# Two equal stationary pieces of 64 columns for the state update and the logits of a scan with two mixtures of experts

## The chip, the cores and the metric

The kernel runs on one core of one Trainium2 chip, in one launch. The metric is the device time of the whole program in microseconds (us), and the median of several runs is quoted. The core's engines are TensorE (PE, with its weight loads shown apart as PEld), VectorE (DVE), ScalarE (ACT), GpSimd (POOL) and SyncE (SP, which issues the transfers here).

## The reference

Three stages follow each other: a linear recurrence with a complex gate (`attn`), a dense two-layer map with a piecewise quadratic function (`moe`), and eight experts with weights from a balanced softmax (`moe2`).

```python
# attn: B, H, S, D = 4, 8, 768, 48; a is scaled so that |a| <= 0.999
for t in range(S):
    new_re = ar * S_re - ai * S_im
    new_im = ar * S_im + ai * S_re
    kv = np.einsum('bhd,bhe->bhde', k[:, :, t], v[:, :, t])
    S_re, S_im = (new_re + kv, new_im)
    y[:, :, t] = np.einsum('bhd,bhde->bhe', q[:, :, t], S_re)
# moe: 3072 tokens, d_model 384, d_ff 2048
h = x @ w_in
g = np.where(h >= 1, h, np.where(h <= -1, 0.0, (h + 1) ** 2 / 4))
x = g @ w_out
# moe2: 8 experts, d_ff 1024
P = np.exp(x @ w_gate - max)      # then 8 rounds of row and column scaling
out = sum over e of P[:, e:e + 1] * (np.maximum(x @ w1[e], 0) @ w2[e])
```

## The kernel before

The 768 steps are cut into six chunks of 128, and the four batches into two pairs; a chunk of one pair is a unit `u`, so there are twelve. A unit has 16 heads (8 for each batch of the pair).

For a unit the front part (`attn_norm`, `attn_front`) scales the gates and forms their running products along time: it turns them with transposes (`tA`), runs a scan of complex products on VectorE (`Pk`, `M`), turns them back (`tP`) and makes scaled queries `qh` and keys `kh` (96 values a head: 48 real, 48 imaginary). The back part (`attn_back`) then works like chunked linear attention:

- `turn(g)` transposes four heads of `kh` and `qh` (`kTps`, `qTps`), and ScalarE copies them out;
- `score(g)` makes the 128x128 scores of four heads (`sc`), and VectorE masks them into `at`;
- `value(g)` makes the output `y` of four heads, from the carried state `Tst` (line 385, not in the first chunk) and from `at` and the values `v` (line 389). Its 128 rows of output are made as two pieces of 64 (`halves`);
- `state(b)` (lines 393 to 402) makes what the chunk adds to the state, `z`, for the 8 heads of one batch: the head's 96 columns of `kh` are the stationary operand, as a piece of 64 and one of 32, and the head's 48 values `v` move. `z` is then added to `Tst`, by ScalarE's copy in the first chunk and by VectorE after that. The last chunk has no state update, which leaves ten units with two blocks each.

At the end of a unit `y` is transposed (`x0ps`) and split into a high and a low part, `x0h` and `x0l`. `moe1(u)` takes them through the first mixture: layer 1 into `h` (line 123), the quadratic on ScalarE and VectorE (`t`, then `gh` and `gl`), layer 2 into `x2pa` and `x2pb` (line 513). Then, for each of three chunks `m` of the model dimension, ScalarE copies 128x256 results out (`x2b`), a transfer stores them, and two matmuls (one for each batch) add to the logits `lg` (line 526), with 128 columns of `x2b` as the stationary and 8 of `w_gate` moving. VectorE copies `lg` to `P`.

`weave` draws pieces of the attention of later units between the matmuls of `moe1(u)`, and a scheduler that sees priorities sets the final order on each engine at build time. Float32 weights of the first mixture arrive as raw words in three staging buffers (`stg`); VectorE repacks them (`st_m`), and a pair of matmuls (`lo`) helps split them. After the twelve units the eight experts run on TensorE (`eh` at line 123, `o` at line 657) to the end. PSUM tiles of the attention and of `lg` share the pool `psp` with three buffers.

Of the kernel before, what the change touches and what calls it, by code (L numbers as in the profile page):

```python
# [9 lines left out]
F32 = mybir.dt.float32  # L10
# [10 lines left out]
def scan_moe_moe(  # L21
# [14 lines left out]
    nc = tc.nc  # L36
    B, H, S, D = q.shape
# [3 lines left out]
    T = 128  # L41
    NCH = S // T
    KC = DM // 128
    NF1 = F1 // 128
    NF2 = F2 // 128
    BH = 2
    NU = NCH * (B // BH)
    HU = BH * H
    CU = BH * DM
    G = CU // 128  # L50
    D2 = 2 * D
# [38 lines left out]
    wg = const.tile([128, KC, NE], F32, name="wg")  # L90
# [7 lines left out]
    def f32(ap):  # L98
        return ap.bitcast(F32)
# [54 lines left out]
            )  # L154
            yield

    # ------------------------------------------------------------------
    # phase 1 pools
    # ------------------------------------------------------------------
    ph1 = ctx.enter_context(ExitStack())  # L160
    wpb = ph1.enter_context(tc.tile_pool(name="wpb", bufs=NF1 - 12))
    x0p = ph1.enter_context(tc.tile_pool(name="x0p", bufs=3))
# [1 line left out]
    ap1 = attn.enter_context(tc.tile_pool(name="ap1", bufs=1, side="right"))  # L164
# [70 lines left out]
    def parts(u):  # L235
        return [(b, 1) for b in range(BH)] if u < NSPLIT else [(0, BH)]

    front = {}

    def attn_front(u):  # L240
        c, bp = divmod(u, B // BH)
        A, qn, kn, vn = (loaded.pop((u, nm)) for nm in "aqkv")
        PN = ap1.tile([128, 2, CU], F32, name=f"PN{u}", tag="PN")
        Pk = ap1.tile([128, 2, G, T], F32, name=f"Pk{u}", tag="Pk")
        M = ap1.tile([128, 2, 2, G, T // 2], F32, name=f"M{u}", tag="s12")
        n12 = ap1.tile([128, 2, CU], F32, name=f"n12_{u}", tag="s12")
        qh = ap1.tile([128, HU, 2, D], F32, name=f"qh{u}", tag="qh")
        kh = ap1.tile([128, HU, 2, D], F32, name=f"kh{u}", tag="kh")
        front[u] = (qh, kh, vn)
        tiles = (A, qn, kn, Pk, M, PN, n12, qh, kh)  # L250
        yield from both(*[front_part(u, c, bp, b0, nb, *tiles) for b0, nb in parts(u)])

# [90 lines left out]

    def attn_back(u):
        c, bp = divmod(u, B // BH)
        qh, kh, vn = front.pop(u)
        qf = qh.rearrange("p h i d -> p h (i d)")
        kf = kh.rearrange("p h i d -> p h (i d)")
        alt = ps_a if u == 0 else psp
        ys = [ap1.tile([128, DM], F32, name=f"ysb{u}_{b}", tag="ysb", bufs=2) for b in range(BH)]  # L350
        NG = HU // 4
        halves = (slice(0, 64), slice(64, 128))
        kqT, ats = {}, {}

        def turn(g):
            tt = []
            for nm, src in (("kT", kf), ("qT", qf)):
                ps = alt.tile([128, 4, 128], F32, name=f"{nm}ps{u}_{g}", tag="m")
                for i in range(4):
                    nc.tensor.transpose(ps[:D2, i, :], src[:, 4 * g + i, :], ident)  # L360
                t = ap1.tile([128, 4, 128], F32, name=f"{nm}{u}_{g}", tag=nm, bufs=2)
                nc.scalar.activation(t[:D2], ps[:D2], AF.Copy)
                tt.append(t)
            kqT[g] = tt

        def score(g):
            kT, qT = kqT[g]
            ps = psp.tile([128, 4, 128], F32, name=f"sc{u}_{g}", tag="m")
            for i in range(4):
                nc.tensor.matmul(ps[:, i, :], kT[:D2, i, :], qT[:D2, i, :], start=True, stop=True)  # L370
            at = ap1.tile([128, 4, 128], F32, name=f"at{u}_{g}", tag="at", bufs=2)
            nc.vector.tensor_tensor(
                out=at, in0=ps, in1=mask.unsqueeze(1).to_broadcast([128, 4, 128]), op=ALU.mult
            )
            ats[g] = at

        def value(g):
            at = ats.pop(g)
            qT = kqT.pop(g)[1]
            yps = psp.tile([128, 4, D], F32, name=f"y{u}_{g}", tag="m")  # L380
            for i in range(4):
                h = 4 * g + i
                if c:
                    for o in halves:
                        nc.tensor.matmul(  # L385
                            yps[o, i, :], qT[:D2, i, o], Tst[:D2, bp * HU + h, :], start=True, stop=False
                        )
                for o in halves:
                    nc.tensor.matmul(yps[o, i, :], at[:, i, o], vn[:, h, :], start=(c == 0), stop=True)  # L389
            o = g % 2 * 4 * D  # L390
            nc.scalar.activation(ys[g // 2][:, o:o + 4 * D], yps.rearrange("p h d -> p (h d)"), AF.Copy)

        def state(b):
            zps = psp.tile([128, H, D], F32, name=f"z{u}_{b}", tag="m")
            for h in range(b * H, (b + 1) * H):
                for o in (slice(0, 64), slice(64, D2)):
                    nc.tensor.matmul(zps[o, h - b * H, :], kf[:, h, o], vn[:, h, :], start=True, stop=True)  # L397
            tv = Tst[:D2, bp * HU + b * H:bp * HU + (b + 1) * H, :]
            if c == 0:
                nc.scalar.activation(tv, zps[:D2], AF.Copy)  # L400
            else:
                nc.vector.tensor_tensor(out=tv, in0=zps[:D2], in1=tv, op=ALU.add)

        turn(0)
        yield 1
        for g in range(NG + 1):
            if g + 1 < NG:
                turn(g + 1)
                yield 1
            if g < NG:  # L410
                score(g)
                yield 1
            if g:
                value(g - 1)
                yield 1
                if g % 2 == 0 and c < NCH - 1:
                    state(g // 2 - 1)
                    yield 1
        xh = x0p.tile([128, KC, UT], F32R, name=f"x0h{u}", tag="x0h")
        xl = x0p.tile([128, KC, UT], F32R, name=f"x0l{u}", tag="x0l")  # L420
        for kcs in ((0, 1), (2,)):
            ps = psp.tile([128, 2, UT], F32, name=f"x0ps{u}_{kcs[0]}", tag="m")
            for kc in kcs:
                for b in range(BH):
                    nc.tensor.transpose(
                        ps[:, kc - kcs[0], b * T:(b + 1) * T], ys[b][:, kc * 128:(kc + 1) * 128], ident
                    )
            n = len(kcs)
            oh = xh[:, kcs[0]:kcs[0] + n, :]
            ol = xl[:, kcs[0]:kcs[0] + n, :]  # L430
            nc.scalar.activation(oh, ps[:, :n], AF.Copy)  # L431
            nc.vector.tensor_tensor(out=ol, in0=ps[:, :n], in1=f32(oh), op=ALU.subtract)  # L432
        x0[u] = (xh, xl)
        yield 1
# [42 lines left out]
    def moe1(u):  # L477
# [4 lines left out]
        for p in range(NP + LAG1):  # L482
# [19 lines left out]
            if p >= LAG1:  # L502
                gh, gl = hh.pop(p - LAG1)
                for i in range(2):
                    j = 2 * (p - LAG1) + i
                    w = wm[j]
                    for m in range(KC):
# [4 lines left out]
                        for n, (s, g) in enumerate(((0, gh), (0, gl), (1, gh))):  # L512
                            nc.tensor.matmul(  # L513
                                acc[m], w2p(w, s, m * 128, 128), g[:, i, :],
                                start=(j == 0 and n == 0 and m != 1), stop=(j == NF1 - 1 and n == 2 and m != 0),
                                skip_group_check=(m < 2),
                            )
                    yield 1
        lg = psp.tile([128, BH, NE], F32, name=f"lg{u}", tag="m")
        for m in range(KC):  # L520
            with tc.high_priority(60):
                xb = x0p.tile([128, UT], F32, name=f"x2b{u}_{m}", tag="x2b", bufs=2)
                nc.scalar.activation(xb, acc[m], AF.Copy, scale=0.25)
                nc.sync.dma_start(x2s[c][:, m, bp * UT:(bp + 1) * UT], xb)
            for b in range(BH):
                nc.tensor.matmul(  # L526
                    lg[:, b, :], xb[:, b * T:(b + 1) * T], wg[:, m, :],
                    start=(m == 0 and b == 0), stop=(m == KC - 1 and b == BH - 1), skip_group_check=True,
                )
        j = c * B + bp * BH  # L530
        nc.vector.tensor_copy(P[:, j:j + BH, :], lg)
        yield 1
# [20 lines left out]
    def both(*gs):  # L553
        gs = list(gs)
        while gs:
            for g in list(gs):
                try:
                    yield next(g)
                except StopIteration:
                    gs.remove(g)  # L560
# [41 lines left out]
    load_qkv(0)  # L602
    drain(attn_norm(0))
    drain(attn_front(0))
    side = chain(*[step(u) for u in range(NU)])
    for u in range(NU):
# [7 lines left out]
        weave(moe1(u), side, RATIO)  # L614
    ph1.close()

    # ------------------------------------------------------------------
    # phase 2
    # ------------------------------------------------------------------
    xrp2 = main.enter_context(tc.tile_pool(name="xrp2", bufs=1, side="right", reuse_waits="tile"))  # L620
    accp = main.enter_context(tc.tile_pool(name="accp", bufs=1, reuse_waits="tile"))
    acc = accp.tile([128, NTT, DM], F32, name="acc")
# [73 lines left out]
    for n in range(len(steps) + LAG):  # L696
        if n < len(steps):
            i, f = steps[n]
# [8 lines left out]
        if n >= LAG:  # L707
            i, f = steps[n - LAG]
# [8 lines left out]
                            j = units[r][1] * B + b  # L717
                            nc.vector.tensor_scalar_mul(acc[:, j, :], acc[:, j, :], P[:, j, 0:1])

    # ------------------------------------------------------------------  # L720
    # inputs outside the ranges that the path above covers
    # ------------------------------------------------------------------
    st = const.tile([128, 4], F32, name="st")
    nc.vector.tensor_reduce(out=st[:, 0:1], in_=mins, axis=AX.X, op=ALU.min)
    nc.vector.reduce_max(out=st[:, 1:2], in_=wst[:, 0], axis=AX.XY)
# [235 lines left out]
```

## Time and profile before

| | us |
|---|---|
| median of 3 runs | 2410.22 |
| lowest, highest | 2409.65, 2413.41 |
| span of the profiled execution | 2408.3 |
| PE busy | 2344.7 |
| DVE busy | 1075.6 |
| ACT busy | 806.6 |
| POOL busy | 1.4 |

The results name no other time for the profiled execution than its span, from the first to the last instruction. A busy time is the union of the records of an engine; PE records overlap, since matmuls are pipelined, so the pace of a row of matmuls is read from the start of one to the start of the next and not from their durations. Each float32 matmul of the program leaves two records. A row of the timeline merges neighbours of one kind: its start, its length, the engine, the line, the tile, the shape of the array used (rows*columns of the stationary), the operand, and the number of records.

### The profile page before, as it was taken

The numbers are of one execution on the slowest core, as the hardware profiler recorded it, in microseconds if no ns is written. First come the engines' busy times: TensorE is split into PE (matmuls) and PEld (weight loads), VectorE is DVE, ScalarE is ACT, GpSimd is POOL, SyncE is SP. The second block draws the span as 40 slices with busy tenths as digits, with TensorE's granted clock in tenths as the row PEclk, the third lists the DMA queues.
The fourth block names the chain that finished last, engine by engine and source line by source line (L and its number), as shares of the span: only waits on it lengthen the run. The fifth ranks groups of instructions, "written<-read, shape, count | busy, mean of one in ns | idle before, by whom it ended". The sixth has DMA issues, their size and how long they took to land.

```text
span 2408.3 us, 34837 instructions
## 1 busy us (share of the span) xinstructions
PE 2344.7 (97%) x14957; PEld 2133.0 (89%) x14957; DVE 1075.6 (45%) x2060; ACT 806.6 (33%) x1405; POOL 1.4 (0%) x14
## 2 busy tenths in 40 slices
PE   4899999999999999999999999999999999999998
PEld 3679999999999898999999999999999999999997
DVE  7788877776665783322322232232232223222222
ACT  5677776665567211211211121121121112111111
POOL 0000000000000000000000000000000000000000
PEclk8999999999999999999999999999999999999999
DMA  6442222221103330100100010010010001000000
GB/s 131 138 93 47 40 41 40 42 45 35 34 15 125 112 133 13 53 1 1 46 7 1 14 40 1 1 53 1 1 47 7 1 16 38 1 1 7 27 27 28
DMA packets 186163, 90.42 MB, mean 38 GB/s; under 512 B 128400, under 2 KB 181136, under 8 KB 186000
## 3 DMA queue, kind: packets, MB, share of 16 engines
q1 hardware_dynamic: 186000, 88.11, 13.9%
q8 instruction: 119, 1.95, 0.3%
q14 instruction: 44, 0.36, 0.1%
HBM read 78.66 MB, written 9.44 MB: 37 GB/s over the span
## 4 chain that ended last, share of the span: by engine, by line
PE 90%; DVE 4%; DMA 3%; ACT 2%; issue 1%; SPq 0%; DVEq 0%; ACTq 0%
PE eh L123 32%; PE o L657 31%; PE h L123 8%; PE x2pa L513 5%; PE z L397 3%; PE x2pb L513 2%; PE sc L370 2%; DMA raw<-in_moe_w_in_dram 2%; PE y L385 1%; PE y L389 1%; PE lo L472 1%; PE qTps L360 1%; PE kTps L360 1%; DVE M L282 1%; PE lg L526 1%
## 5 line engine op out<-in xcount | busy, mean ns | idle before, releaser
L123 PE MATMUL eh<-x2h,w_e 128*128 128x512 f32 x2304 | 783.3, 394 | 0.0
L657 PE MATMUL o<-w_e,eg 128*128 128x384 f32 x3072 | 780.5, 334 | 0.7 <-DVE acc L667 0.7
L643 DVE SCALAR_TENSOR_TENSOR el<-eh,eg 128x512 fp32r<-128x512 f32 x384 | 264.9, 690 | 895.9 <-ACT eg L642 895.9
L642 ACT ACTIVATE eg<-eh 128x512 fp32r<-128x512 f32 x384 | 229.6, 598 | 1248.1 <-PE eh L123 1229.2
L657 PEld LDWEIGHTS o<-w_e,eg 128*128 128x128 f32 x3072 | 560.7, 188 | 35.9 <-issue 0.9
L657 PE MATMUL o<-w_e,el 128*128 128x384 f32 x1536 | 513.8, 335 | 0.0
L123 PEld LDWEIGHTS eh<-x2h,w_e 128*128 128x128 f32 x2304 | 432.9, 188 | 83.8
L123 PE MATMUL eh<-x2l,w_e 128*128 128x512 f32 x1152 | 456.9, 397 | 0.0
L657 PEld LDWEIGHTS o<-w_e,el 128*128 128x128 f32 x1536 | 288.4, 188 | 0.0
L123 PEld LDWEIGHTS eh<-x2l,w_e 128*128 128x128 f32 x1152 | 216.2, 188 | 34.7
L123 PE MATMUL h<-x0h,w_m 128*128 128x256 f32 x1152 | 233.1, 290 | 1.0 <-ACT x0h L431 0.5
L123 PEld LDWEIGHTS h<-x0h,w_m 128*128 128x128 f32 x1152 | 186.9, 192 | 3.7 <-issue 1.1
L513 PE MATMUL x2pa<-gh,w_m 128*128 128x256 f32 x768 | 179.7, 295 | 9.3 <-ACT gh L498 9.3
L123 PE MATMUL h<-x0l,w_m 128*128 128x256 f32 x576 | 163.7, 284 | 0.1
L671 DVE SCALAR_TENSOR_TENSOR acc<-o,P,acc 128x384 f32<-128x384 f32 x168 | 95.5, 611 | 128.7 <-PE o L657 128.7
L513 PEld LDWEIGHTS x2pa<-gh,w_m 128*128 128x128 f32 x768 | 134.6, 193 | 13.1 <-ACT gh L498 11.0
L123 PEld LDWEIGHTS h<-x0l,w_m 128*128 128x128 f32 x576 | 110.8, 192 | 0.5 <-DVE x0l L432 0.3
L513 PE MATMUL x2pa<-gl,w_m 128*128 128x256 f32 x384 | 111.2, 289 | 0.1
L513 PE MATMUL x2pb<-gh,w_m 128*128 128x256 f32 x384 | 101.5, 284 | 0.0
L110 DVE TENSOR_TENSOR w_e<-st_e,w_e 128x768 fp32r<-128x768 f32 x64 | 61.1, 957 | 79.9 <-ACT w_e L109 79.9
L492 ACT ACTIVATE t<-h,c_one 128x512 f32<-128x512 f32 x96 | 65.8, 685 | 56.8 <-PE h L123 49.0
L109 ACT ACTIVATE w_e<-st_e 128x768 fp32r<-128x768 f32 x64 | 53.9, 844 | 79.1 <-PE o L657 75.6
(135 smaller groups left out, 2184.2 us busy)
## 6 DMA issues: line engine op xcount, KB each, us to landing
st_e<-in_moe_w_dram SPq DMA_DIRECT2D x128, 192.0 KB, 2.6
st_m<-in_moe_w_in_dram SPq DMA_DIRECT2D x16, 384.0 KB, 3.6
st_m<-in_moe_w_out_dram SPq DMA_DIRECT2D x16, 384.0 KB, 4.2
raw<-in_moe_w_in_dram SPq DMA_DIRECT2D x16, 384.0 KB, 3.5
raw<-in_moe_w_out_dram SPq DMA_DIRECT2D x16, 384.0 KB, 4.0
q<-in_q_dram SPq DMA_DIRECT2D x12, 384.0 KB, 4.0
k<-in_k_dram SPq DMA_DIRECT2D x12, 384.0 KB, 3.7
v<-in_v_dram SPq DMA_DIRECT2D x12, 384.0 KB, 3.7
```

Source lines behind the costliest of these rows:

```text
L109: nc.scalar.activation(w[:, 0, :], st, AF.Copy)
L110: nc.vector.tensor_tensor(out=w[:, 1, :], in0=st, in1=f32(w[:, 0, :]), op=ALU.subtract)
L123: nc.tensor.matmul(ps, w1p(w, s, kc), x[:, kc, :], start=(n == 0), stop=(n == 3 * KC - 1))
L360: nc.tensor.transpose(ps[:D2, i, :], src[:, 4 * g + i, :], ident)
L370: nc.tensor.matmul(ps[:, i, :], kT[:D2, i, :], qT[:D2, i, :], start=True, stop=True)
L397: nc.tensor.matmul(zps[o, h - b * H, :], kf[:, h, o], vn[:, h, :], start=True, stop=True)
L492: nc.scalar.activation(t, ps, AF.Relu, bias=c_one, scale=-0.25)
L513: nc.tensor.matmul(acc[m], w2p(w, s, m * 128, 128), g[:, i, :], start=(j == 0 and n == 0 and m != 1), stop=(j == NF1 - 1 and n == 2 and m ...
L642: nc.scalar.activation(xh, ps, AF.Relu)
L643: nc.vector.scalar_tensor_tensor(out=xl, in0=ps, scalar=0.0, in1=f32(xh), op0=ALU.max, op1=ALU.subtract)
L657: nc.tensor.matmul(po[i, b], g[:, b * T:(b + 1) * T], w2p(w, s, 0, DM), start=(f == 0 and n == 0), stop=(f == NF2 - 1 and n == 2),)
L671: nc.vector.scalar_tensor_tensor(out=a, in0=ps, scalar=P[:, j, e:e + 1], in1=a, op0=ALU.mult, op1=ALU.add)
```

## The change

The stationary operand of the state update becomes two pieces of 64 columns a head. The second piece begins at the head's column 64 and goes 32 columns past its end, into the next head's columns; the results of those 32 columns land in partitions 96 to 127 of `z`, which nothing reads. For the last head the tile of `kh` is 32 columns longer, and GpSimd clears these with a memset for each unit. The logits' matmuls are cut in two along the tokens, 64 columns of `x2b` each. The rest of the diff replaces comments by blank lines.

```diff
         qh = ap1.tile([128, HU, 2, D], F32, name=f"qh{u}", tag="qh")
-        kh = ap1.tile([128, HU, 2, D], F32, name=f"kh{u}", tag="kh")
-        front[u] = (qh, kh, vn)
+        khx = ap1.tile([128, HU * D2 + 32], F32, name=f"kh{u}", tag="kh")
+        nc.gpsimd.memset(khx[:, HU * D2:], 0.0)
+        kh = khx[:, :HU * D2].rearrange("p (h i d) -> p h i d", h=HU, i=2)
+        front[u] = (qh, khx, vn)
...
-        qh, kh, vn = front.pop(u)
+        qh, khx, vn = front.pop(u)
         qf = qh.rearrange("p h i d -> p h (i d)")
-        kf = kh.rearrange("p h i d -> p h (i d)")
+        kf = khx[:, :HU * D2].rearrange("p (h m) -> p h m", h=HU)
...
             for h in range(b * H, (b + 1) * H):
-                for o in (slice(0, 64), slice(64, D2)):
-                    nc.tensor.matmul(zps[o, h - b * H, :], kf[:, h, o], vn[:, h, :], start=True, stop=True)
+                for o in halves:
+                    ko = khx[:, h * D2 + o.start:h * D2 + o.stop]
+                    nc.tensor.matmul(zps[o, h - b * H, :], ko, vn[:, h, :], start=True, stop=True)
...
             for b in range(BH):
-                nc.tensor.matmul(
-                    lg[:, b, :], xb[:, b * T:(b + 1) * T], wg[:, m, :],
-                    start=(m == 0 and b == 0), stop=(m == KC - 1 and b == BH - 1), skip_group_check=True,
-                )
+                for o in (0, 64):
+                    nc.tensor.matmul(
+                        lg[o:o + 64, b, :], xb[:, b * T + o:b * T + o + 64], wg[:, m, :],
+                        start=(m == 0 and b == 0), stop=(m == KC - 1 and b == BH - 1), skip_group_check=True,
+                    )
```

TensorE at the first state update of unit 7, between two layer-2 pieces of unit 6, before the change (a row gives the line, the tile written, the operands and the shape of the output; a number behind a name is the unit, the last one a buffer):

```order
L513 MATMUL x2pb6_5474<-gl6_3_5546,w_m6_707 128x256
L513 MATMUL x2pb6_5474<-gh6_3_5545,w_m6_707 128x256
L397 MATMUL z7_0_5737<-v7_4574,kh7_4607 64x48
L397 MATMUL z7_0_5737<-v7_4574,kh7_4607 32x48
...
L513 MATMUL x2pa6_5473<-gh6_3_5545,w_m7_733 128x256
L513 MATMUL x2pa6_5473<-gl6_3_5546,w_m7_733 128x256
```

The same place after the change:

```order
L516 MATMUL x2pb6_5519<-gl6_3_5591,w_m6_708 128x256
L516 MATMUL x2pb6_5519<-gh6_3_5590,w_m6_708 128x256
L400 MATMUL z7_0_5782<-v7_4611,kh7_4644 64x48 x16
L516 MATMUL x2pa6_5518<-gh6_3_5590,w_m7_734 128x256
L516 MATMUL x2pa6_5518<-gl6_3_5591,w_m7_734 128x256
```

The block stands where it stood, with 16 matmuls as before; the eight of 32 columns have become eight of 64.

TensorE at the logits of unit 6, which stand among the first layer-1 matmuls of unit 7, before:

```order
L123 MATMUL h7_0_6042<-x0h7_5946,w_m0_531 128x256
L526 MATMUL lg6_6012<-wg_96,x2b6_0_6013 128x8 x2
L123 MATMUL h7_0_6042<-x0h7_5946,w_m0_531 128x256
L123 MATMUL h7_0_6042<-x0l7_5947,w_m0_531 128x256
L526 MATMUL lg6_6012<-wg_96,x2b6_1_6018 128x8 x2
L123 MATMUL h7_0_6042<-x0h7_5946,w_m0_531 128x256 x2
```

and after:

```order
L123 MATMUL h7_0_6093<-x0h7_5991,w_m0_532 128x256
L530 MATMUL lg6_6057<-wg_96,x2b6_0_6058 64x8 x4
L123 MATMUL h7_0_6093<-x0h7_5991,w_m0_532 128x256
L530 MATMUL lg6_6057<-wg_96,x2b6_1_6065 64x8 x4
L123 MATMUL h7_0_6093<-x0l7_5992,w_m0_532 128x256
```

Two matmuls of 128 columns have become four of 64, and the second group stands one layer-1 matmul earlier. Elsewhere on TensorE and VectorE some neighbours change places by one or a few instructions. GpSimd has twelve memsets more, each waiting for TensorE's last use of the unit before; VectorE's write of `kh` waits for GpSimd besides, and so does the last matmul of a unit's second state block.

## Rows read from the trace of the kernel before

**Rows 1.** Page: busy time of engines, and the chain by engine and line

```profile
PE 2344.7 (97%) x14957; PEld 2133.0 (89%) x14957; DVE 1075.6 (45%) x2060; ACT 806.6 (33%) x1405; POOL 1.4 (0%) x14
...
PE 90%; DVE 4%; DMA 3%; ACT 2%; issue 1%; SPq 0%; DVEq 0%; ACTq 0%
PE eh L123 32%; PE o L657 31%; PE h L123 8%; PE x2pa L513 5%; PE z L397 3%; PE x2pb L513 2%; PE sc L370 2%; DMA raw<-in_moe_w_in_dram 2%; PE y L385 1%; PE y L389 1%; PE lo L472 1%; PE qTps L360 1%; PE kTps L360 1%; DVE M L282 1%; PE lg L526
```

**Rows 2.** Waits of PE, 200 to 700 us: total, times, longest

```profile
PE h L123 <- DVE t L495: 0.2, 1, 0.2
```

**Rows 3.** Timeline of PE, first state block of unit 7: start, length

```profile
505.67 3.65 PE L397 MATMUL z<-v,kh 128*64 128x48 f32 x32
509.25 0.39 PE L513 MATMUL x2pa<-gh,w_m 128*128 128x256 f32 x1
```

**Rows 4.** Windows around the twenty z blocks, z alone: first window and sum

```profile
57.90:62.00 4.10, 3.62 (x32) 2.63 (x32) 0.00 (x0) 0.15 (x1) 1.00 0.00 0
...
sum 79.70, PE 73.06 PEld 52.66 DVE 1.56 ACT 0.50; mean PE 3.65 PEld 2.63 DVE 0.08 ACT 0.02
```

**Rows 5.** Timeline of PE, a y block of unit 7 with its neighbours

```profile
493.64 0.28 PE L513 MATMUL x2pb<-gh,w_m 128*128 128x256 f32 x1
493.85 0.32 PE L385 MATMUL y<-Tst,qT 96*64 96x48 f32 x4
...
494.70 0.29 PE L389 MATMUL y<-v,at 128*64 128x48 f32 x4
494.92 0.39 PE L123 MATMUL h<-x0h,w_m 128*128 128x256 f32 x1
495.14 0.28 PE L123 MATMUL h<-x0l,w_m 128*128 128x256 f32 x1
```

**Rows 6.** Windows after three z blocks; the granted clock follows POOL's entry

```profile
224.70:227.80 3.10, 3.10 (x17) 3.06 (x16) 2.95 (x5) 0.05 (x1) 0.00 (x0) 0.53 0.64 126
285.50:289.00 3.50, 3.50 (x18) 3.44 (x18) 2.50 (x5) 1.34 (x3) 0.00 (x0) 0.52 0.57 112
509.20:512.70 3.50, 3.50 (x31) 3.45 (x30) 3.34 (x8) 1.59 (x3) 0.00 (x0) 1.00 0.02 5
```

**Rows 7.** Timeline of PE, a logits group among layer-1 matmuls

```profile
474.57 0.28 PE L123 MATMUL h<-x0l,w_m 128*128 128x256 f32 x1
474.69 0.51 PE L526 MATMUL lg<-wg,x2b 128*128 128x8 f32 x4
475.05 0.48 PE L123 MATMUL h<-x0h,w_m 128*128 128x256 f32 x2
475.37 0.28 PE L123 MATMUL h<-x0l,w_m 128*128 128x256 f32 x1
```

**Rows 8.** Chain in unit 0; timeline of DVE and PE in unit 1

```profile
58.37 3.44 PE z L397 x32
...
64.45 3.42 PE z L397 x32
...
69.53 0.68 PE lo L472 x2
...
166.34 0.69 DVE L372 TENSOR_TENSOR at<-sc,mask 128x512 f32<-128x512 f32 x1 [1.98 <-PE sc L370]
...
172.52 0.69 DVE L432 TENSOR_TENSOR x0l<-x0ps,x0h 128x512 fp32r<-128x512 f32 x1 [1.32 <-ACT x0h L431]
...
179.93 1.50 PE L263 MATMUL tP<-ident,Pk 128*128 128x128 f32 x12 [0.41 <-DVE Pk L291]
```

**Rows 9.** Timeline of DVE and PE around the two z blocks of unit 7

```profile
509.36 0.55 DVE L402 TENSOR_TENSOR Tst<-z,Tst 96x384 f32<-96x384 f32 x1 [0.40 <-PE z L397]
...
513.05 0.69 DVE L372 TENSOR_TENSOR at<-sc,mask 128x512 f32<-128x512 f32 x1
...
516.97 0.32 PE L385 MATMUL y<-Tst,qT 96*64 96x48 f32 x4
...
524.07 0.55 DVE L402 TENSOR_TENSOR Tst<-z,Tst 96x384 f32<-96x384 f32 x1 [4.49 <-PE z L397]
```

## The prediction

> **What bounds the kernel now.** I read the page first. TensorE is busy for 2344.7 of 2408.3 us, and the chain of work that ended last is 90% PE, with z, the state update, on it for 3% of the span [rows 1]. That share is 72 us, so time taken out of z is time on the path as long as nothing else becomes late. Next I asked for PE's waits from 200 to 700 us, where the attention and the first mixture of experts are woven and sixteen of the twenty z blocks lie. The answer is one row of 0.2 us [rows 2]: nothing holds PE up there. VectorE and ScalarE run beside it with slack that has to be measured, which is done below. The later experts, eh and o, have 63% of the chain [rows 1] and the change does not touch them.
>
> The pair of rows to look at is one z block: 32 records (each float32 matmul leaves two) from the start at 505.67 to the next plain matmul at 509.25, which is 3.58 us or 0.112 us a record [rows 3]. All twenty blocks look so: windows around each hold 32 records, 73.06 us busy in sum [rows 4]. The y block does the same kind of work (stationary pieces of 64 columns, 48 moving columns) and has 32 records as well; the first 28 take from 493.85 to 494.70, 0.030 us a record [rows 5]. So z runs nearly four times slower per record than y. What differs is the width: y alternates 64 and 64 columns, z alternates 64 and 32.
>
> **The state update.** From its start to the next plain matmul a y block takes 493.85 to 494.92, 1.07 us [rows 5]; the z block takes 3.58 [rows 3]. The changed z has y's shape in every number of the form (64 columns, 48 moving, 128 rows of contraction), so I take y's price: 2.51 us less for a block, 20 x 2.51 = 50.2 us. The bounds are nothing gained (the pieces keep 0.112) and little more than 2.51.
>
> The Trainium skill (TensorEngine Tiling (Array Packing), Key Properties) says that changing the tiling mode, not just the tile, drains TensorE. It names no price; the two rows differ in the way that rule would have them differ. The skill also has a rule against this change (TensorE: Matmul & The Clock Gate, LDWEIGHTS): a load takes as many cycles of 1.2 GHz as the stationary has columns. The second piece grows from 32 to 64 columns, and an estimate by that formula is 53 ns a record. By the page a z block would come down to about 1.8 us and the blocks would give 35 us; by the rows it is 50. The y records at 30 ns disagree with that formula for two halves in turn, and the measurement decides.
>
> The 32 zero columns behind kh cost one memset a unit on GpSimd. That engine has 14 instructions in the whole trace [rows 1], and in the order the memset stands behind the state update of the unit before, well ahead of kh's write. I cost it and the new waits on it at nothing. The cover is GpSimd's idleness; without it kh, and the transposes behind it, would be late by one memset.
>
> **The clock.** Twice the granted clock is 0.52 to 0.53 of full, its level of 1.2 GHz, right after a z block, while it is 1.00 after the block at 505 [rows 6]. PE had run z for 3.6 us just before, and no stretch after a y block from 200 to 700 us shows it. The two stretches lose 3.10 x 0.47 = 1.5 and 3.50 x 0.48 = 1.7 us of full clock, 3.1 together. With z at 1 us I count both as gone. The other bound is that they stay or move elsewhere: 0.
>
> **The logits.** Here the change adds width changes where there were none. 36 groups of four records with 128 columns, each between plain 128-column matmuls, become 36 groups of eight records with 64. One group now takes, with its neighbours, 474.57 to 475.37, 0.80 us, less three plain steps of 0.12: 0.44 [rows 7]. The ends of a y block cost, from the plain matmul before (493.64) to the second after (495.14), 1.50 less 0.24 for two plain steps and 0.96 for 32 records: 0.30 [rows 5]. So after the change a group costs 8 x 0.030 + 0.30 = 0.54, which is +0.10 each and +3.6 us in all. No row has 64 columns against 8 moving ones, so the bounds are wide. Below: 0.24 with a third of the ends, 0.34, gives -4 us. Above: loads that do not overlap, half of the present 0.36 / 4 = 0.09 a record [rows 7], give 8 x 0.045 + 0.30 = 0.66, +8 us. The skill's drain rule speaks against this half of the change and has the same sign.
>
> **Where a gain may be lost.** In unit 0 both z blocks are on the chain, and what follows them there is PE's own lo for the next weights [rows 8]. It all moves up, and I count 5 us in full. In unit 1 it does not. VectorE has unit 2's scan to do and idles only 1.98 us for the scores and 1.32 us at x0l, and tP already waits 0.41 us for that scan [rows 8]. So the scan can end 3.3 us sooner but PE come 5.0 sooner: 1.7 us are lost.
>
> In units 2 to 9 VectorE is dense around the first z block. At 509 us it idles 0.40 us for z, so it gains 0.4 where PE gains 2.5, and the 2.1 us must be slack elsewhere. The closest need is at: it starts at 513.05 and takes 0.69, and its y starts at 516.97 [rows 9]. That is 3.2 us of slack, of which 1.1 is left. At the second z block VectorE idles 4.49 us waiting for z itself [rows 9], so there it moves up with PE. I take no loss here, but this is the thinnest cover.
>
> **The sum** against the profiled execution: 2408.3 - 50.2 - 3.1 + 3.6 + 1.7 = 2360.3 us of span. The results give no separate time for that execution. Its span is 1.9 us below the median of the three runs (2410.22), which I add: 2362.2 us, 2.0% faster.
>
> **The rivals.** First, VectorE becomes the bound. If the 1.1 us above is not there in units 2 to 9 (a wait that is hidden now, or an instruction or two that the changed order puts ahead of at), the first z block of each gives 0.4 instead of 2.5: 8 x 2.1 = 17 us lost, 2379. For it: VectorE's dense stretch. Against: the slack just read, and PE's wait of 0.2 us in 500. Chance 0.10.
>
> Second, the new pieces load without the overlap that y has, at the 0.045 us a record of the upper bound above. Then a z block keeps 32 x 0.015 = 0.48 us more, 10 us in all, and the logits cost 8 instead of 3.6: 2377. Against: y's records. Chance 0.04. (The page's load formula is this mechanism; at its 53 ns the time would be some 2383.)
>
> Third, on the slow side: the change doesn't do what it says, since the pause belongs to going from one half of the array to the other with kh as the stationary, not to unequal widths. Then z keeps 0.112 us a record and the logits take that pace too: 8 x 0.112 + 0.30 = 1.20 a group, 36 x 0.76 = 27 us more, 2437. In general, with p us a record for both, the state gains 640 x (0.112 - p) and the logits lose 36 x (8p - 0.14), so the kernel is slower only from p = 0.083. y alternates halves at 0.030 and speaks against it. Chance 0.02.
>
> **How the numbers follow.** The forecast has the remaining 0.84. Its own bounds: below, logits at -4 and nothing lost in unit 1, 2410.2 - 50.2 - 3.1 - 4 = 2353; above, logits at +8, the clock dips kept and 5 us lost in units 0 and 1, 2410.2 - 50.2 + 8 + 5 = 2373. To hold 8 in 10 the range takes in these and reaches into the first two rivals, where only some units lose: 2353 to 2377. A measurement of this kernel can tell about 0.2%, 5 us, from no change. Faster by more than that: forecast and first two rivals, 0.97 with a point left aside. Within it: 0.01, a pace near 0.083. Slower: 0.02.
>
> **What would show it.** In the profile after: z blocks of 32 records that take about 1.1 us, with one form of 64 columns; no granted clock near 0.5 after a z block; logits groups of eight records near 0.54 us; PE's waits still near nothing between 200 and 700 us. VectorE's idle time at the second z block should fall from 4.49 to about 2 us. If PE waits for at, Pk or kh in every unit instead, the first rival holds. If the z records keep 0.1 us, the third does, and the forecast is wrong.

## The result and the profile after

The median went from 2410.32 to 2359.61 us, a ratio of 0.9787 with a 95% interval of [0.9774, 0.9799]. The forecast was 2362 us, in a range of 2353 to 2377. The span of the profiled execution went from 2408.3 to 2356.7 us, 51.6 us less.

The page of the changed kernel has 53.5 us less of TensorE's busy time. On the chain of work that ended last, `z` held 3% [rows 1] and is no longer among the lines that the page has room for; VectorE's share has gone from 4% to 8%, which the part on VectorE below comes back to. Engines with busy time, share and instructions, then the chain:

```profile
PE 2291.2 (97%) x15101; PEld 2093.2 (89%) x15101; DVE 1075.0 (46%) x2060; ACT 805.2 (34%) x1405; POOL 2.9 (0%) x26
...
PE 86%; DVE 8%; ACT 3%; DMA 2%; issue 1%; SPq 0%; DVEq 0%; ACTq 0%
```

The timeline of TensorE at the first state block of unit 7, the place of [rows 3]: start, length, line, tile, shape and records.

```profile
470.43 0.28 PE L516 MATMUL x2pb<-gh,w_m 128*128 128x256 f32 x1
470.64 1.14 PE L400 MATMUL z<-v,kh 128*64 128x48 f32 x32
471.71 0.39 PE L516 MATMUL x2pa<-gh,w_m 128*128 128x256 f32 x1
```

From start to the next plain matmul the block takes 1.07 us for the same 32 records; it took 3.58. That is the time of the y block [rows 5], to the hundredth.

The logits of unit 6, which answer to [rows 7], two groups with one layer-1 matmul between them and then a lone one:

```profile
438.56 0.28 PE L123 MATMUL h<-x0h,w_m 128*128 128x256 f32 x1
438.86 0.41 PE L530 MATMUL lg<-wg,x2b 128*64 128x8 f32 x8
439.19 0.38 PE L123 MATMUL h<-x0h,w_m 128*128 128x256 f32 x1
439.51 0.40 PE L530 MATMUL lg<-wg,x2b 128*64 128x8 f32 x8
439.84 0.39 PE L123 MATMUL h<-x0l,w_m 128*128 128x256 f32 x1
440.06 0.40 PE L123 MATMUL h<-x0h,w_m 128*128 128x256 f32 x2
...
442.21 0.40 PE L123 MATMUL h<-x0h,w_m 128*128 128x256 f32 x2
442.54 0.40 PE L530 MATMUL lg<-wg,x2b 128*64 128x8 f32 x8
442.88 0.39 PE L123 MATMUL h<-x0l,w_m 128*128 128x256 f32 x1
443.10 0.40 PE L123 MATMUL h<-x0h,w_m 128*128 128x256 f32 x2
```

The waits of TensorE from 180 to 680 us (total, times, longest), which answer to [rows 2], have one row, and it is a new one: the transposes `tP` wait for VectorE's `x0l`. In the timeline the three places stand behind the state blocks of units 2, 3 and 4:

```profile
PE tP L265 <- DVE x0l L435: 2.2, 3, 0.9
```

```profile
215.94 1.09 PE L265 MATMUL tP<-ident,Pk 128*128 128x128 f32 x8 [0.48 <-DVE x0l L435]
...
271.67 1.09 PE L265 MATMUL tP<-ident,Pk 128*128 128x128 f32 x8 [0.94 <-DVE x0l L435]
...
327.06 1.09 PE L265 MATMUL tP<-ident,Pk 128*128 128x128 f32 x8 [0.78 <-DVE x0l L435]
```

The next fence is VectorE and TensorE between the two state blocks of unit 7, as in [rows 9]. The masked scores `at` end at 478.26 and their `y` starts at 479.43, so 1.2 us of slack is left. At the second state block VectorE idles 0.26 us where it idled 4.49.

```profile
477.58 0.68 DVE L374 TENSOR_TENSOR at<-sc,mask 128x512 f32<-128x512 f32 x1
...
479.43 0.32 PE L387 MATMUL y<-Tst,qT 96*64 96x48 f32 x4
...
484.06 0.55 DVE L405 TENSOR_TENSOR Tst<-z,Tst 96x384 f32<-96x384 f32 x1 [0.26 <-PE z L400]
```

Behind both blocks of that unit TensorE has its full granted clock (the entry after POOL's is 1.00, the level of 2.4 GHz), and so has every window of 10 us from 200 to 760 us; before, two of them had fallen [rows 6].

```profile
471.70:475.20 3.50, 3.50 (x33) 3.49 (x30) 3.50 (x6) 2.03 (x5) 0.00 (x0) 1.00 0.00 0
483.90:487.40 3.50, 3.50 (x33) 3.49 (x30) 1.94 (x3) 1.76 (x3) 0.12 (x1) 1.00 0.57 112
```

A good ruler for a late unit is the distance between two starts of `x0ps`, since TensorE waits for nothing there: from 433.14 to 487.25 it is 54.11 us, and before it was 59.12 (468.18 to 527.30).

```profile
433.14 0.82 PE L428 MATMUL x0ps<-ident,ysb 128*128 128x128 f32 x6
...
487.25 0.82 PE L428 MATMUL x0ps<-ident,ysb 128*128 128x128 f32 x6
```

### The profile page after: what moved, and what is told of

Read it like the earlier page. It is cut to its first block, busy times and chain, and to the rows that moved or that the text cites. A ratio compares the mean times of both kernels' runs of the same rounds, so it can differ in the third digit from the quotient of the medians.

```text
span 2356.7 us, 35161 instructions
## 1 busy us (share of the span) xinstructions
PE 2291.2 (97%) x15101; PEld 2093.2 (89%) x15101; DVE 1075.0 (46%) x2060; ACT 805.2 (34%) x1405; POOL 2.9 (0%) x26
## 4 chain that ended last, share of the span: by engine, by line
PE 86%; DVE 8%; ACT 3%; DMA 2%; issue 1%; SPq 0%; DVEq 0%; ACTq 0%
PE eh L123 32%; PE o L661 32%; PE h L123 7%; PE x2pa L516 4%; PE x2pb L516 2%; DMA raw<-in_moe_w_in_dram 2%; DVE M L284 1%; PE sc L372 1%; PE lo L475 1%; DVE M L289 1%; DVE Pk L293 1%; PE y L387 1%; PE kTps L362 1%; PE y L391 1%; PE qTps L362 1%
```

## The experiments

The theory was that a change between a 64-column and a 32-column stationary is what the state update paid for, and that the logits matter little. The rivals were that the logits gave a part, that a 32-column piece or the operand `kh` is slow in itself, and that the gain came from a second piece as wide as y's and not from equal pieces.

**The state update alone.** The changed kernel with the logits as before:

```diff
-                for o in (0, 64):
-                    nc.tensor.matmul(
-                        lg[o:o + 64, b, :], xb[:, b * T + o:b * T + o + 64], wg[:, m, :],
+                nc.tensor.matmul(
+                    lg[:, b, :], xb[:, b * T:(b + 1) * T], wg[:, m, :],
```

> State update in equal pieces of 64, logits whole (128 columns) as before the change. Theory (going between a 64- and a 32-column piece is what z paid for; the logits' own change is small): z blocks of 1.07 us from start to next plain matmul, as in the changed kernel, and a time of 2359 us, within 2 us of the changed kernel. By the prediction's own price for the logits (+3.6 us) this kernel would be 3 to 4 us faster than the changed one, 2356. Rival (a good part of the gain came from the logits): 2370 us or more.

2362.35 us, ratio 0.9795 [0.9781, 0.9808]. In the timeline of its TensorE two starts of `x0ps` are 54.07 us apart:

```profile
436.37 0.82 PE L428 MATMUL x0ps<-ident,ysb 128*128 128x128 f32 x6
490.44 0.82 PE L428 MATMUL x0ps<-ident,ysb 128*128 128x128 f32 x6
```

So the state update has all of the gain, as far as these runs can tell, and cutting the logits costs 0.04 us a unit, not the 0.3 us that the prediction had. The median is above the changed kernel's, inside both intervals. Its profiled execution had lost 2.6 us by the first state block (start at 59.2 us, against 56.6 in the changed kernel), before any edited instruction had run.

**The logits alone.** The kernel before with only the logits cut:

```diff
-                nc.tensor.matmul(
-                    lg[:, b, :], xb[:, b * T:(b + 1) * T], wg[:, m, :],
+                for o in (0, 64):
+                    nc.tensor.matmul(
+                        lg[o:o + 64, b, :], xb[:, b * T + o:b * T + o + 64], wg[:, m, :],
```

> Logits in two pieces of 64 columns, state update as before the change (64 and 32). Theory: z blocks stay at 3.58 us, the time stays within 2 us of before, 2409 to 2413 us. The prediction's price gives 2414. Rival (the logits gain by themselves): below 2405.

2411.32 against 2410.74 us, ratio 1.0004 [0.9995, 1.0013]: no difference that can be measured, and +3.6 us (1.0015) lies outside the interval. This kernel still has z blocks of 3.6 us, and from 200 us on one window of 10 us in it has a fallen clock again. The fall to 0.50, the level of 1.2 GHz, lasts from 273.0 to 276.5 us, right behind a state block that starts at 269.2:

```profile
270.00:280.00 10.00, 10.00 (x96) 9.05 (x95) 7.99 (x15) 4.33 (x9) 0.00 (x0) 0.83 0.01 2
```

**The same pieces in another order.** The kernel before, unequal pieces kept, all of one width first:

```diff
-            for h in range(b * H, (b + 1) * H):
-                for o in (slice(0, 64), slice(64, D2)):
+            for o in (slice(0, 64), slice(64, D2)):
+                for h in range(b * H, (b + 1) * H):
```

> Before the change, but a state block does the 64-column pieces of all 8 heads first and then the 32-column pieces of all 8: the same 32 records with the same shapes and loads, one change of width inside instead of fifteen. Theory (the change of width is the price): a block of 1.1 to 2.2 us, since only the overlap of two halves may be missing, and a time of 2360 to 2382 us. Rival (a 32-column piece is slow in itself, whatever stands beside it): the 16 records of the 32-column pieces keep about 0.19 us each, a block of 3 us or more and a time over 2395 us.

2373.57 us, ratio 0.9846 [0.9831, 0.9861]. The first fence is one block in the timeline of TensorE; the second groups all records of z by form (busy time, mean ns):

```profile
546.78 1.93 PE L397 MATMUL z<-v,kh 128*64 128x48 f32 x32
548.64 0.39 PE L513 MATMUL x2pa<-gh,w_m 128*128 128x256 f32 x1
```

```profile
L397 PE MATMUL z<-v,kh 128*64 128x48 f32 x320 | 22.5, 224 | 0.0
L397 PE MATMUL z<-v,kh 128*32 128x48 f32 x320 | 17.4, 208 | 0.0
```

A block takes 1.86 us instead of 3.58, with the same instructions and operands. So the 32-column piece is not slow in itself, and three quarters of what the change gave come from the order alone. The rest is something that this order cannot give. In each of the 20 blocks the 16 records of 64 columns are busy for 22.5 / 20 = 1.13 us; less the 0.22 of the last one, that is 0.90 for 15 steps or 0.060 us a record, all at one place of the array. Where two places alternate, in `y` and in the changed `z`, it is 0.030. By these paces pieces at the same place take turns, and pieces at two places overlap.

**Three equal pieces of 32.** The kernel before with one edit; no column with unread results, no memset:

```diff
-                for o in (slice(0, 64), slice(64, D2)):
+                for o in (slice(0, 32), slice(32, 64), slice(64, D2)):
```

> The kernel before, with the head's 96 columns as three pieces of 32: equal pieces again, but no column whose result is unread, no longer tile of kh and no memset; 48 records a block instead of 32. Theory (unequal widths are the price): 48 records at 0.025 to 0.044 us, a block of 1.2 to 2.1 us, a time of 2360 to 2381 us. Rival (what helped was that the second piece got as wide as y's, 64 columns, not that the pieces are equal): 0.1 us a record, a block of 4 us or more and a time no better than before.

2364.22 us in a single run. The block in the timeline of TensorE:

```profile
379.90 0.88 PE L397 MATMUL z<-v,kh 128*32 128x48 f32 x48
380.71 0.39 PE L513 MATMUL x2pa<-gh,w_m 128*128 128x256 f32 x1
```

48 records take 0.81 us, 0.017 us each, less than the theory allowed. The rival falls: width 64 is not what matters. Equal pieces matter, and with three places that alternate a record takes less than with two. A block is 0.26 us shorter than in the changed kernel, so this kernel was run five times more:

> Three pieces of 32 columns for the state, logits whole, timed. In its first look a z block took 0.81 us against 1.07 in the changed kernel and a late unit 53.6 us against 54.1, but units 2 to 4 waited 4.5 us for VectorE and the clock fell once. If the late units decide: 5 us below the changed kernel, 2355 us. Rival (VectorE in the early units takes back what the shorter blocks give): 2359 to 2364 us.

2363.01 us, ratio 0.9799 [0.9785, 0.9814], so the rival of this run held: it is not faster than the changed kernel. A late unit takes 53.6 us, 0.5 less, but the early ones give it back. The waits of its TensorE from 180 to 720 us, and a window of 10 us of it:

```profile
PE tP L263 <- DVE x0l L432: 4.5, 3, 1.9
PE h L123 <- DVE t L495: 0.7, 1, 0.7
```

```profile
270.00:280.00 10.00, 8.11 (x56) 7.81 (x55) 6.67 (x11) 8.27 (x16) 0.00 (x0) 0.83 0.12 23
```

The wait at `tP` doubled from 2.2 us, and in unit 3, behind a wait of 1.89 us that ends at 275.65, the granted clock fell to 0.50 from 276.5 to 279.5 us.

**Unequal pieces put into y.** The changed kernel with the scores' part of `y` cut 64, 32, 32:

```diff
-                for o in halves:
+                for o in (slice(0, 64), slice(64, 96), slice(96, 128)):
                     nc.tensor.matmul(yps[o, i, :], at[:, i, o], vn[:, h, :], start=(c == 0), stop=True)
```

> The changed kernel, with the scores' half of y (line 391) in pieces of 64, 32 and 32 columns: two changes of width for each head, 32 a unit, put where there were none. Theory: each costs 0.12 to 0.16 us, as in z (2.51 us for sixteen of them, or 1.92 us where the loss of overlap is taken out), so 12 x 32 x 0.12 to 0.16 = 46 to 61 us, and some 10 us for 32 more records a unit: 2405 to 2435 us. Rival (the price belongs to the stationary kh of the state update): only the further records, below 2375 us.

2413.89 us in a single run, where nine runs of the kernel before the change lie between 2408.69 and 2417.22: the whole gain is gone. A y block in the timeline:

```profile
515.43 0.32 PE L387 MATMUL y<-Tst,qT 96*64 96x48 f32 x4
515.58 0.49 PE L391 MATMUL y<-v,at 128*64 128x48 f32 x6
516.00 0.32 PE L387 MATMUL y<-Tst,qT 96*64 96x48 f32 x4
...
517.29 0.49 PE L391 MATMUL y<-v,at 128*64 128x48 f32 x6
517.71 0.38 PE L123 MATMUL h<-x0h,w_m 128*128 128x256 f32 x1
```

It takes 2.28 us where it took 1.07 [rows 5]. With 0.24 for the eight further records at 0.030, 0.97 us stay. Inside the block there are seven more changes of width (two a head, but the last piece is followed by plain matmuls, as it was before), 0.14 us each. The price is not bound to `kh` or to the state update: it appears in `y` as soon as the widths are mixed there.

**The state block right behind the y block.** The state-only kernel without matmuls between the two:

```diff
                 value(g - 1)
-                yield 1
                 if g % 2 == 0 and c < NCH - 1:
                     state(g // 2 - 1)
                     yield 1
+                yield 1
```

> State update in equal pieces, logits whole, and the state block put right behind the y block, without layer-2 or layer-1 matmuls between them. y and z are then one stretch of 64-column pieces, with one way in and one way out less for each of the twenty blocks (four of them stood so already). By the price of the ends read before (0.30 us for in and out) 16 x 0.30 = 4.8 us less than the state-only kernel: 2354 us. Rival (the ends are hidden or VectorE is late for the next steps): the same as the state-only kernel within 1.5 us.

2359.69 us, ratio 0.9790 [0.9776, 0.9803], 2.7 us under the state-only kernel, inside its interval. Then once more beside the changed kernel:

> The changed kernel once more, beside the next one on the same chip. 2358 to 2363 us. If the logits' cut costs 0.06 us a unit, as the state-only kernel's 54.05 us a unit against 54.11 says, nothing of it can be seen in the time.

> The state block right behind the y block (logits whole) once more, beside the changed kernel on the same chip. It was 2.7 us below the state-only kernel where the ends alone would have given 4.8, since TensorE had new short waits for VectorE. Theory: 2 to 3 us below the changed kernel. Rival (that difference was the start of the program, whose clock differs from run to run): no difference beyond 1.5 us.

The changed kernel had 2360.13 us, 0.9787 [0.9772, 0.9801]; the adjacent one 2360.48 us, 0.9786 [0.9772, 0.9800]. The rival held: no difference. One reason is new waits of TensorE, 180 to 720 us:

```profile
PE tP L265 <- DVE x0l L435: 1.6, 3, 1.2
PE z L400 <- DVE at L374: 0.8, 1, 0.8
PE x2pa L516 <- DVE gl L502: 0.7, 2, 0.3
PE x2pa L516 <- ACT gh L501: 0.6, 1, 0.6
PE h L123 <- DVE t L498: 0.4, 1, 0.4
```

These are 4.1 us against 2.3 in the changed kernel, which takes back 1.8 of the 4.8 us that the ends (going from plain matmuls into 64-column pieces and out again) should give. The ruler shows the rest. From unit 5 to unit 9 a unit takes 53.75 us on average, 0.32 less than the 54.07 of the state-only kernel and not the 0.60 of two pairs of ends; and the unit between `x0ps` of units 4 and 5 takes 56.80 instead of 55.03. From `x0ps` of unit 1 to that of unit 9 only 0.2 us of gain are left. Why a late unit, which hardly waits, gives half of the price is open.

**The scores cut too.** The changed kernel, `score` in two pieces:

```diff
-                nc.tensor.matmul(ps[:, i, :], kT[:D2, i, :], qT[:D2, i, :], start=True, stop=True)
+                for o in halves:
+                    nc.tensor.matmul(ps[o, i, :], kT[:D2, i, o], qT[:D2, i, :], start=True, stop=True)
```

> The changed kernel, with the scores (line 372) also in two pieces of 64 columns: 16 records of 128 moving columns a group where there were 8. They take 0.81 us now, at 0.10 a record. Theory (loads and matmuls of two halves overlap, as in y and z, and what is left is the 128 columns that move, 0.05 a record in two halves at once): 16 x 0.03 + 0.30 for the ends = 0.78, no difference, 2359 to 2361 us. Rival (the halves take turns at the moving columns): 16 x 0.053 + 0.30 = 1.15 us a group, 48 x 0.34 = 16 us more, 2376.

2370.29 us, ratio 0.9828 [0.9814, 0.9841], some 10 us slower than the changed kernel. A group in the timeline of the changed kernel, and then one here:

```profile
473.97 1.05 PE L372 MATMUL sc<-qT,kT 96*128 96x128 f32 x8
474.78 0.36 PE L123 MATMUL h<-x0h,w_m 128*128 128x256 f32 x1
```

```profile
482.57 1.09 PE L373 MATMUL sc<-qT,kT 96*64 96x128 f32 x16
483.59 0.39 PE L123 MATMUL h<-x0h,w_m 128*128 128x256 f32 x1
```

16 records of 128 moving columns take 1.02 us where 8 took 0.81; with the ends, counted as in the prediction, it is 1.22 against 0.89, near the rival's 1.15 and far from the theory's 0.78. Here the halves gain nothing: a record takes 0.064 us, and there are twice as many. That a record keeps the array for its moving columns fits this (a plain matmul moves 256 columns in 0.12 us, so 128 in 0.06), but it does not fit the three pieces of 32, whose 0.017 us is less than 48 columns at that pace, 0.022. Why the halves of the scores do not overlap stays open. Late units are 1.22 us longer, 14.6 us for twelve, of which some 4 are hidden, mostly in the early units, where TensorE's wait at `tP` falls from 2.2 to 0.3 us.

## Why the prediction was right, and where not

**The state update** was right, 2.51 us a block: 1.07 us is y's price. Done alone it has the whole gain, and without it there is none. The reason given for it, unequal widths, was shown from both sides, by taking the changes of width out of `z` without touching the pieces and by putting them into `y`. The grouped kernel adds a second part that the prediction did not take apart, the overlap of the halves: 0.79 of the 2.51 us.

**The clock** was right as far as it can be seen, and a little too dear. The two falls behind z blocks are not there after the change. From 200 us on, of the other kernels, the one with long z blocks and cut logits has a fall behind a block, and the one with three pieces has one behind its longest wait; the state-only, grouped, adjacent, uneven-y and cut-scores kernels have none. Only three of the 32 long blocks from 200 us on, in the kernel before and the logits-only one, are followed by a fall, so what else it takes is not shown. Before 200 us every kernel has falls, at differing places. The price can be read for the first fall: from `x0ps` of unit 1 to that of unit 2 the kernel before takes 58.12 us and the logits-only kernel, which has no fall there, 56.70, so it cost 1.4 of the forecast 1.5. For the second (1.7) the nearest pair is the kernel before, whose next unit is 1.99 us above its late ones, and the uneven-y kernel, where it is 0.89 above without a fall: some 1.1.

**The logits** are the term that was mis-sized: +3.6 us, and it is about +0.5 (0.04 us a unit by the ruler, twelve units; the medians of the logits-only run differ by 0.6, which is inside the interval). The lone group costs what was worked out: from the second layer-1 matmul of the pair at 442.21, which starts at 442.33, to the pair at 443.10 is 0.77, less two steps of 0.12, 0.53 us. The step that failed is taking one group's 0.44 us before for all 36. The first group of a unit also waited for its operand, ScalarE's copy `x2b`, and cost 0.72 (473.61 to 474.57, less two steps), and after the change the second stands one layer-1 matmul behind the first. The two cost 1.16 us together before and 1.14 after. The changed order was printed ahead of the prediction and was not priced.

```profile
473.61 0.28 PE L123 MATMUL h<-x0h,w_m 128*128 128x256 f32 x1
473.90 0.61 PE L526 MATMUL lg<-wg,x2b 128*128 128x8 f32 x4
```

**Unit 0 and unit 1** were right. The first state block starts 1.6 us earlier than before, `x0ps` of unit 0 6.6 us, so unit 0 gave 5.0. From the first state block of unit 1 to `tP` the gain grew by 3.4 us (161.60 to 155.28, then 179.93 to 170.20), where the two blocks give 5.0: 1.6 us lost to VectorE's scan, 1.7 had been forecast.

**VectorE in units 2 to 9** was counted at nothing and cost 2.2 us, at another place than the one watched. The slack at `at` is 1.2 us, as worked out (1.1). The wait came at `tP`, whose PSUM buffer must be freed by `x0l`, in units 2 to 4. That is the first rival at an eighth of its size, but VectorE did become the bound there: the chain of the changed kernel runs mostly over VectorE from 143 to 327 us, where before it was almost wholly TensorE's from 199 us on. Its pieces at the last of the three waits (start, length, what):

```profile
325.24 0.69 DVE gl L502
...
326.40 0.61 DVE x0l L435
327.06 1.09 PE tP L265 x8
```

So in these units VectorE now sets the pace and TensorE has nothing more to give, and the shorter z blocks with three pieces show how it goes on. VectorE's idle time at the second block fell to 0.26 us and not to 2: the 2.1 us that VectorE lags after the first block had to be taken from it as well, a step left out of a detail that the sum did not use. The memsets on GpSimd cost nothing that the waits of TensorE show, as forecast.

**The sum.** By these measures the span should fall by 50.2 + 3.1 - 0.5 - 1.6 - 2.2 = 49.0 us; it fell by 51.6. 1.6 us of the difference are the start, before any state block. There TensorE's granted clock from 50 to 60 us was 0.83 before and 0.97 after, and it differs from run to run: the first state block starts at 59.2 us with 0.73 (the state-only kernel), 58.2 with 0.83, 57.8 with 0.86 (the changed kernel's second trace) and 56.6 with 0.97. The window of before, and of the changed kernel:

```profile
50.00:60.00 10.00, 10.00 (x97) 9.16 (x96) 6.56 (x11) 7.21 (x15) 0.00 (x0) 0.83 0.18 31
```

```profile
50.00:60.00 10.00, 9.72 (x147) 9.13 (x147) 7.71 (x14) 8.70 (x18) 0.00 (x0) 0.97 0.11 18
```

At `x0ps` of unit 9 the gain is 50.05 us, 0.6 less than the terms up to there with the start (50.7), which is about what the clock was too dear. Behind it another 1.5 us arise, 1.3 of them between the first and the last matmul of `eh`, which the change does not touch; why stays open. That the forecast came within 3 us is in part luck: the logits were 3.1 us too dear and VectorE's waits 2.2 us too cheap, which nearly cancel, and the start and the end, which were not forecast, gave 3.1.

## What to carry to other kernels

Cut small stationaries into equal pieces, even if some columns are computed for nothing. Of two neighbouring blocks on TensorE compare start-to-start time per record, not duration: z and y both had a median of 222 ns and ran at 0.112 and 0.030 us. Equal pieces paid where few columns move (48 here); cutting an uncut stationary in two where 128 move only doubled the records. Before counting the gain, walk the other engine's order past the shortened block and look at every buffer that it frees. Look at the chain after the change as well: where it has gone over to another engine, the next cut on this one gives nothing.

## What the runs showed of the hardware

- A change between 64- and 32-column stationaries costs 0.12 to 0.17 us on TensorE: in `z` 0.12 against grouped pieces ((3.58 - 1.86) / 14 fewer changes) and 0.17 against equal ones ((3.58 - 1.07) / 15), in `y` 0.14 (0.97 / 7). The drain of which the Trainium skill speaks (TensorEngine Tiling (Array Packing), Key Properties) agrees with these, and this would be its price here.
- Pieces of 64 columns and 48 moving columns take 0.060 us a record in a row at one place and 0.030 when two places alternate, and pieces of 32 take 0.017 when three places do. The Trainium skill's load formula (TensorE: Matmul & The Clock Gate, LDWEIGHTS) gives 53 ns for 64 columns; that is near the first figure, and alternating places go below it. For 32 columns in a row an estimate by the formula is 27 ns, and the grouped kernel has 0.044 us ((17.4 / 20 - 0.21) / 15), so there it is too low.
- With 128 moving columns two alternating places show no such gain: 1.02 us for 16 records of 64 columns, 0.064 each, against 0.81 for 8 of 128 columns.
